# Gated GQA decode step with a gMLP branch: the last head's V load is merged, wo is cut into four loads, and dummy matmuls move

## Chip, cores and metric

One core of a Trainium2 chip runs the whole kernel. The metric is the device time of one execution in microseconds (us); the time of a kernel is the median of several runs.

## The reference, cut to what matters

One token `x` (1 x 1024) goes through two branches that a scalar gate mixes.

```python
def _A_ref(x, k_cache, v_cache, wq, wo):          # 32 query heads, 4 KV heads, 65536 keys, 128 per head
    q = (x @ wq).reshape(B, Sq, Hq, Dh).transpose(0, 2, 1, 3)
    k = jnp.repeat(k_cache, rep, axis=1)           # rep = 8
    v = jnp.repeat(v_cache, rep, axis=1)
    scores = jnp.einsum('bhqd,bhkd->bhqk', q, k) * Dh ** (-0.5)
    p = _softmax(scores, axis=-1)
    o = jnp.einsum('bhqk,bhkd->bhqd', p, v)
    return o.transpose(0, 2, 1, 3).reshape(B, Sq, Hq * Dh) @ wo
...
g = _sigmoid((x * gate_w).sum(-1, keepdims=True))
a = _A_ref(x, A_k_cache, A_v_cache, A_wq, A_wo)
b = _B_ref(x, B_w_in, B_w_sp, B_b_sp, B_w_out)     # a small gMLP block on the same token
return g * a + (1 - g) * b
```

All inputs are bfloat16. The K and V caches are 64 MB each; `wq` and `wo` are 8 MB each, `w_in` 7 MB and `w_out` 3.5 MB. There is one token, so every byte of them is read once and used little.

## The kernel before

**The buffer.** Everything large is loaded by SP's queue (`load`, L177 to L187, issue on L184) into one SBUF buffer `kv` of five slots of 4 MB. A slot holds one tile of a cache: 128 partitions times 128 keys times 128 values. A load names its slot by `at`, which may be a fraction. A load waits until the instructions that used the slot before are done. SP issues in program order, so the order of the loads is written out by hand.

**K tiles** (`k_tile`, L407 on). Each KV head has four K tiles. VectorE (DVE) transposes a tile in place in four parts (L412), TensorE (PE) multiplies it with the query weights `wt` (L419, 32 matmuls of 512 columns), ScalarE (ACT) copies the scores to SBUF (L428). `stats` (L431 on) takes the maximum, the exponentials and their sums and transposes the probabilities into `pt` (L454).

**V tiles** (`v_tile`, L457 on). A V tile needs nothing of DVE: 32 matmuls of 512 columns (L464) with 64 columns of `pt` as weights add to the PSUM tile `o_ps`. After a head's four V tiles `head_out` (L472 on) masks and sums `o_ps` on DVE (L474, L478), adds up over partitions by small matmuls (L482, L484), divides by the softmax sums, multiplies by the gate and writes the head's part of `oa` (L487 to L496).

**The order.** For heads 1 to 3, pairs of K tiles of one head alternate with pairs of V tiles of the head before (L529 to L548). The last head's V tiles come at the end (L549 to L551): tiles 0 and 1 in one load into slots 2 and 3, tile 2 alone into slot 1, tile 3 alone into slot 0. Slots 0 and 1 held V tiles 2 and 3 of the head before.

**The end.** `project` (L511 on) multiplies rows of `wo` with `oa` into `out_ps`: four matmuls of 256 columns (L514) for each of 32 rows, each with a weight load of its own. `wo` comes in as many loads as `WO_SPLIT` has entries, from slot 3 on; so the first, of 24 rows, waits until V tile 1 of the last head has been used. The other loads lie in the upper half of slot 4. Then ACT copies `out_ps` (L566), and two queues write it out (L569).

**Dummy matmuls.** `keep_busy(n)` (L499 to L506) issues `n` matmuls of 512 columns with one weight load (L503) on data that lies in SBUF; their result is never read. Before, there are 6 ahead of the last `head_out`, 16 behind it, and `WO_BUSY[n]` of them behind the `project` of a piece of `n` rows of `wo`.

**Order on each engine.** At the end of the program every instruction is tied to the one before it on its engine (L572 to L579), so each engine runs exactly in the order in which the code is written.

Of the kernel before, what the change touches and what calls it, by code (L numbers as in the profile page):

```python
# [21 lines left out]
CC = CT // VC  # L22
ZN = 448
HN = 512
WO_SPLIT = (24, 4, 2, 1, 1)
WO_BUSY = {24: 0, 4: 2, 2: 1, 1: 0}


@with_exitstack
def kernel(  # L30
# [18 lines left out]
    _, G, S, DH = A_k_cache.shape  # L49
# [15 lines left out]
    assert S % (P * CT) == 0 and F == 2 * NB * ZN and ZN == B * FC and HD == NHB * NB * HN  # L65
    assert NHB * NB == 2 * G and CC * B == 2 * HN and sum(WO_SPLIT) == OC

# [12 lines left out]
    def same_weights(ins):  # L80
        held.add(ins.ins.name)
# [95 lines left out]
    def load(src, shape, at):  # L177
        n = 1
        for s in shape:
            n *= s  # L180
        v = kv[:, int(at * CT * P):int(at * CT * P) + n]
        if len(shape) == 2:
            v = v.rearrange("p (a b) -> p a b", b=shape[1])
        ins = nc.sync.dma_start(out=v, in_=src)  # L184
        if not first_load:
            first_load.append(ins.ins.name)
        return v  # L187

    def load_kv(src, g, j, at, n=1):
        h, i = divmod(j, 2)  # L190
        rows = src[0, g, 2 * h * CT * P:2 * (h + 1) * CT * P, :].rearrange(
            "(p c) d -> p (c d)", c=2 * CT)
        v = load(rows[:, i * CT * DH:(i + n) * CT * DH], (n * CT * DH,), at)
        return [v[:, i * CT * DH:(i + 1) * CT * DH] for i in range(n)]
# [166 lines left out]
    for k in range(NHB):  # L361
# [3 lines left out]
                                                                   j=B, e=2),  # L365
# [91 lines left out]
    def v_tile(g, j, vt):  # L457
        if j == 0:
            o_ps[g] = pso.tile([P, 2, VC * DH], FP32, name="o_ps")
        vx = vt.rearrange("p (v c d) -> p c v d", v=VC, d=DH)  # L460
        for u in range(CC // 2):
            hs = slice(u % 2 * P // 2, (u % 2 + 1) * P // 2)
            for e in range(2):
                ins = nc.tensor.matmul(  # L464
                    o_ps[g][hs, e, :],
                    lhsT=ptt[g, j][:, 2 * u:2 * u + 2, :].rearrange("p c x -> p (c x)"),
                    rhs=vx[:, 2 * u + e], start=(j == 0 and u < 2),
                    stop=(j == NT - 1 and u >= CC // 2 - 2), skip_group_check=True)
                if e > 0:
                    same_weights(ins)  # L470

    def head_out(g):  # L472
        gs = slice(g * B, (g + 1) * B)
        nc.vector.tensor_tensor(  # L474
            out=om8, in0=o_ps[g][:].rearrange("p e (v d) -> p (e v) d", d=DH),
            in1=own_8[:].unsqueeze(2).to_broadcast([P, 2 * VC, DH]), op=ALU.mult)
        o_sb = wk.tile([P, DH], FP32, name="o_sb")
        nc.vector.tensor_reduce(out=o_sb[:], in_=om8.rearrange("p x d -> p d x"), axis=AX.X,  # L478
                                op=ALU.add)
        om_ps = psm.tile([P, DH + NT], FP32, name="om_ps", tag="m")  # L480
        hs = hsel[:].rearrange("p h q -> p (h q)")
        nc.tensor.matmul(om_ps[gs, DH:], lhsT=hs, rhs=lss[g][:], start=True, stop=True,  # L482
                         skip_group_check=True)
        nc.tensor.matmul(om_ps[gs, :DH], lhsT=hs, rhs=o_sb[:], start=True, stop=True,  # L484
                         skip_group_check=True)
        rl = wk.tile([P, 2], FP32, name="rl")
        nc.vector.reduce_sum(out=rl[gs, 0:1], in_=om_ps[gs, DH:], axis=AX.X)  # L487
        nc.vector.reciprocal(out=rl[gs, 1:2], in_=rl[gs, 0:1])
        om = wk.tile([P, QD, OC], FP32, name="om")
        nc.vector.tensor_tensor(  # L490
            out=om[gs], in0=om_ps[gs, :DH].rearrange("p (q c) -> p q c", c=OC),
            in1=own_q[gs, :].unsqueeze(2).to_broadcast([B, QD, OC]), op=ALU.mult)
        osum = wk.tile([P, OC], FP32, name="osum")
        nc.vector.tensor_reduce(out=osum[gs, :], in_=om[gs].rearrange("p q c -> p c q"),
                                axis=AX.X, op=ALU.add)
        nc.vector.tensor_scalar(out=oa[gs, :], in0=osum[gs, :], scalar1=rl[gs, 1:2],  # L496
                                scalar2=gate[gs, :], op0=ALU.mult, op1=ALU.mult)

    def keep_busy(n):  # L499
        ps = pss.tile([P, 2 * HN], FP32, name="busy_ps", tag="s")  # L500
        w = wt[G % 2][:].rearrange("p v b t u h -> p (v b t u h)")
        for i in range(n):
            ins = nc.tensor.matmul(ps[:, :HN], lhsT=w[:, :P], rhs=w[:, :HN], start=True,  # L503
                                   stop=True, skip_group_check=True)
            if i > 0:
                same_weights(ins)  # L506
# [4 lines left out]
    def project(w, n, vec, c0, first=False, last=False):  # L511
        for c in range(n):
            for t in range(NB):
                nc.tensor.matmul(  # L514
                    out_ps[t * B:(t + 1) * B, :],
                    lhsT=vec[:, c0 + c:c0 + c + 1].to_broadcast([P, B]),
                    rhs=w[:, c, t * NO:(t + 1) * NO],
                    start=(first and c == 0), stop=(last and c == n - 1),
                    skip_group_check=True)
# [9 lines left out]
    for g in range(1, G):  # L529
# [16 lines left out]
            if h == 0 and g + 1 < G:  # L546
                build_w(g + 1)
        head_out(g - 1)  # L548
    for j, n, at in ((0, 2, 2), (2, 1, 1), (3, 1, 0)):  # L549
        for i, vt in enumerate(load_kv(A_v_cache, G - 1, j, at, n)):  # L550
            v_tile(G - 1, j + i, vt)  # L551
    keep_busy(6)
    head_out(G - 1)
    keep_busy(16)

# [2 lines left out]
    c0 = 0  # L558
    for n in WO_SPLIT:
        t = load(wo_view[:, c0:c0 + n, :], (n, D), 3 + c0 * D / (CT * P))  # L560
        project(t, n, oa, c0, last=(c0 + n == OC))
        keep_busy(WO_BUSY[n])
        c0 += n
# [46 lines left out]
```

## Time and profile before

| what | value |
|---|---|
| median of 6 runs | 381.89 us (381.71 to 382.03) |
| the profiled execution: its own time | 381.77 us |
| its span in the trace | 380.2 us |
| moved over the span | 162.17 MB, 426 GB/s |
| SP's queue, share of 16 DMA engines' span | 98.8% |
| PE busy / DVE busy / ACT busy | 225.9 / 211.2 / 39.6 us |
| mean granted PE clock | 0.834 |

The span runs from the first to the last instruction of the profiled execution; 1.57 us of its time lie outside it. Times in the views below count from the span's start. "Idle before" or a bracket with an arrow names what ended an engine's wait. The granted clock is 1.00 for PE at full speed and 0.50 for half. Matmuls are pipelined, so their mean duration (411 ns for L464) is longer than the distance from one to the next.

The last landings as the trace tells them by what waited for them: V tiles 0 and 1 at 339.22, tile 2 by 348.93, tile 3 at 358.64, the 24 rows of `wo` at 373.16, the last row at 378.14. The V loads were issued at 312.07 (tiles 0 and 1) and from 330.81 on (tiles 2 and 3), the five `wo` loads from 348.71 to 350.94.

### The profile page before, as it was taken

Reading aid. Unit: us, or ns where it says so; the run is one execution under the profiler, and the core shown is the slowest. Engines: PE = TensorE matmul, PEld = TensorE weight load, DVE = VectorE, ACT = ScalarE, POOL = GpSimd, SP = SyncE. Lnnn points to the kernel's source line nnn. Section 1 sums busy time; section 2 is a strip of 40 time slices with the busy share of each in tenths; the row PEclk is TensorE's granted clock in tenths of the full one; section 3 lists DMA queues with packets and bytes.
Section 4 is the critical chain, followed back from the end, with each engine's and each line's share of the span. In section 5 each row is a group of like instructions: output and inputs, shape, how many; then the busy total and the mean of one; then the engine's idle time right before and its main releaser. Section 6 shows DMA issues by size and latency. Waiting matters only on the chain.

```text
span 380.2 us, 2602 instructions
## 1 busy us (share of the span) xinstructions
PE 225.9 (59%) x1397; PEld 55.4 (15%) x800; DVE 211.2 (56%) x207; ACT 39.6 (10%) x55; POOL 4.4 (1%) x10
## 2 busy tenths in 40 slices
PE   0050604967746794794499229762993197739386
PEld 0010100211201210121022001110220011202113
DVE  4152217989474946867893058679940397650040
ACT  1001000111103300114011001140110010500000
POOL 4000000000000000000000000000000000000000
PEclk9995655999958796999599758996899589959889
DMA  9998999999999999999999999999999999999995
GB/s 386 483 434 379 415 442 441 434 480 437 400 408 434 441 436 441 427 441 441 434 436 441 441 434 434 393 429 442 427 441 429 421 441 442 436 403 438 424 439 229
DMA packets 3655, 162.17 MB, mean 426 GB/s; under 512 B 440, under 2 KB 444, under 8 KB 828
## 3 DMA queue, kind: packets, MB, share of 16 engines
q1 hardware_dynamic: 3604, 162.01, 98.8%
q8 instruction: 8, 0.13, 0.1%
q14 instruction: 3, 0.02, 0.0%
q10 hardware_dynamic: 40, 0.01, 0.0%
HBM read 162.01 MB, written 0.00 MB: 426 GB/s over the span
## 4 chain that ended last, share of the span: by engine, by line
DMA 64%; PE 19%; DVE 12%; issue 3%; ACT 1%; SPq 0%; ACTq 0%; DVEq 0%
DMA kv<-in_A_k_cache_dram 45%; PE s_ps L419 14%; DVE kv L412 10%; DMA kv<-in_A_wo_dram 7%; DMA kv<-in_A_v_cache_dram 7%; DMA wb<-in_B_b_sp_dram 5%; PE o_ps L464 3%; DVE pt L454 1%; PE z_ps L296 1%; DVE o_sb L478 0%; SPq L184 0%; DVE mx L402 0%; ACT sc L451 0%; DVE rowt L474 0%; ACT sc L428 0%
## 5 line engine op out<-in xcount | busy, mean ns | idle before, releaser
L419 PE MATMUL s_ps<-kv,wt 128*128 128x512 bf16 x512 | 133.1, 415 | 80.7 <-DVE kv L412 80.6
L412 DVE STREAM_TRANSPOSE kv<-kv 128x2048 int32<-128x2048 int32 x64 | 142.4, 2280 | 69.3 <-DMA kv<-in_A_k_cache_dram 69.3
L464 PE MATMUL o_ps<-kv,pt 128*64 128x512 bf16 x512 | 64.1, 411 | 14.2 <-DMA kv<-in_A_v_cache_dram 14.2
L419 PEld LDWEIGHTS <-wt 128*128 128x128 bf16 x256 | 26.4, 103 | 188.8 <-issue 117.3
L428 ACT CAST sc<-s_ps 128x1024 bf16<-128x1024 f32 x16 | 16.2, 1012 | 252.4 <-PE s_ps L419 252.4
L464 PEld LDWEIGHTS <-pt 128*64 128x64 bf16 x256 | 17.0, 118 | 58.0 <-issue 48.7
L454 DVE STREAM_TRANSPOSE pt<-sc 128x1024 bf16<-128x1024 bf16 x16 | 18.6, 1217 | 6.8 <-ACT sc L451 6.8
L474 DVE TENSOR_TENSOR rowt<-o_ps,own 128x1024 f32<-128x1024 f32 x4 | 4.8, 1195 | 26.8 <-PE o_ps L464 26.8
L451 ACT ACTIVATE sc<-sc,nb 128x1024 bf16<-128x1024 bf16 x16 | 18.2, 1138 | 12.2 <-DVE nb L447 12.2
L484 PE MATMUL om_ps<-o_sb,hsel 128*32 128x128 f32 x8 | 2.3, 386 | 18.3 <-DVE o_sb L478 18.3
L402 DVE TENSOR_TENSOR mx<-mx,sc 128x1024 bf16<-128x1024 bf16 x8 | 5.5, 687 | 13.7 <-ACT sc L428 13.7
L296 PE MATMUL q_ps<-kv,xT 128*32 128x512 bf16 x64 | 6.0, 555 | 8.9 <-DMA kv<-in_A_wq_dram 8.9
L363 DVE TENSOR_TENSOR rowt<-q_ps,own_b 128x512 f32<-128x512 f32 x2 | 1.3, 687 | 12.7 <-PE q_ps L296 12.7
L252 PE MATMUL xb_ps<-xg,spread 8*128 8x256 bf16 x1 | 0.4, 368 | 13.3 <-DMA xg<-in_gate_w_dram 13.3
L478 DVE TENSOR_REDUCE o_sb<-rowt 128x128 f32<-128x1024 f32 x4 | 7.5, 1871 | 0.1
L503 PE MATMUL busy_ps<-wt 128*128 128x512 bf16 x25 | 6.1, 381 | 0.0
L566 ACT CAST out_sb<-out_ps 128x256 bf16<-128x256 f32 x1 | 0.4, 372 | 46.4 <-PE out_ps L514 46.4
L256 DVE TENSOR_TENSOR xm<-xb_ps,sel_i 128x128 f32<-128x128 f32 x2 | 0.5, 286 | 8.1 <-PE xb_ps L252 8.1
L435 DVE TENSOR_REDUCE m<-mx 128x1 f32<-128x1024 bf16 x4 | 4.8, 1210 | 0.1
L514 PE MATMUL out_ps<-kv,oa 128*32 128x256 bf16 x128 | 4.2, 273 | 1.1 <-DMA kv<-in_A_wo_dram 1.1
L296 PEld LDWEIGHTS <-xT 128*32 128x32 bf16 x64 | 2.5, 130 | 15.7 <-issue 15.7
L296 PE MATMUL z_ps<-kv,xT 128*32 128x448 bf16 x64 | 4.7, 464 | 0.0
(90 smaller groups left out, 60.9 us busy)
## 6 DMA issues: line engine op xcount, KB each, us to landing
kv<-in_A_v_cache_dram SPq DMA_DIRECT2D x2, 4096.0 KB, 22.7
kv<-in_B_w_in_dram SPq DMA_DIRECT2D x1, 7168.0 KB, 19.5
kv<-in_A_wo_dram SPq DMA_DIRECT2D x1, 6144.0 KB
kv<-in_B_w_out_dram SPq DMA_DIRECT2D x1, 3584.0 KB
kv<-in_A_wo_dram SPq DMA_DIRECT2D x1, 1024.0 KB, 26.6
kv<-in_A_wo_dram SPq DMA_DIRECT2D x1, 512.0 KB
kv<-in_A_wo_dram SPq DMA_DIRECT2D x2, 256.0 KB
kv<-in_A_k_cache_dram SPq DMA_DIRECT2D x8, 27.5
```

The lines of the kernel that those rows point to most:

```text
L296: ins = nc.tensor.matmul(ps[t * B:(t + 1) * B, k * HN:k * HN + n], lhsT=xT[:, i * KH + c:i * KH + c + 1].to_broadcast([P, B]), rhs=w[:, c, ...
L402: nc.vector.tensor_tensor(out=mx[:], in0=mxs[g][:], in1=sc[:], op=ALU.max)
L412: nc.vector.transpose(out=kb[:, v * n:(v + 1) * n], in_=kb[:, v * n:(v + 1) * n])
L419: ins = nc.tensor.matmul(s_ps[:, k * HN:(k + 1) * HN], lhsT=wt[g % 2][:, v, b].rearrange("p a v h -> p (a v h)"), rhs=kx[:, b // 2, b % 2, ...
L428: nc.scalar.copy(out=sct[g, j][:], in_=s_ps[:])
L435: nc.vector.reduce_max(out=m1[:], in_=mxs[g][:], axis=AX.X)
L451: nc.scalar.activation(out=sct[g, j][:], in_=sct[g, j][:], func=ACT.Exp, scale=SCALE, bias=nb[:, 0:1], accum_out=lss[g][:, j:j + 1])
L454: nc.vector.transpose(out=ptt[g, j][:].rearrange("p c x -> p (c x)"), in_=sct[g, j][:])
L464: ins = nc.tensor.matmul(o_ps[g][hs, e, :], lhsT=ptt[g, j][:, 2 * u:2 * u + 2, :].rearrange("p c x -> p (c x)"), rhs=vx[:, 2 * u + e], sta ...
L474: nc.vector.tensor_tensor(out=om8, in0=o_ps[g][:].rearrange("p e (v d) -> p (e v) d", d=DH), in1=own_8[:].unsqueeze(2).to_broadcast([P, 2 ...
L478: nc.vector.tensor_reduce(out=o_sb[:], in_=om8.rearrange("p x d -> p d x"), axis=AX.X, op=ALU.add)
L503: ins = nc.tensor.matmul(ps[:, :HN], lhsT=w[:, :P], rhs=w[:, :HN], start=True, stop=True, skip_group_check=True)
```

## The change

The last head's V tiles 2 and 3 come in one load of 8 MB, into slots 0 and 1. `wo` comes in 24, 6, 1 and 1 rows, no longer in 24, 4, 2, 1 and 1. Twenty-four dummy matmuls are issued behind V tile 1. The 6 ahead of the last `head_out` and the 16 behind it stay. Behind the 24 rows of `wo` come 2 dummies where there were none, and behind the later pieces none where there were 2 and 1. DVE, ACT and POOL run the same instructions in the same order; PE runs as many `project` matmuls as before.

```diff
@@ -22,8 +22,8 @@
-WO_SPLIT = (24, 4, 2, 1, 1)
-WO_BUSY = {24: 0, 4: 2, 2: 1, 1: 0}
+WO_SPLIT = (24, 6, 1, 1)
+WO_BUSY = {24: 2, 6: 0, 1: 0}
@@ -546,10 +546,10 @@
         head_out(g - 1)
-    for j, n, at in ((0, 2, 2), (2, 1, 1), (3, 1, 0)):
-        for i, vt in enumerate(load_kv(A_v_cache, G - 1, j, at, n)):
+    for j, at in ((0, 2), (2, 0)):
+        for i, vt in enumerate(load_kv(A_v_cache, G - 1, j, at, 2)):
             v_tile(G - 1, j + i, vt)
-    keep_busy(6)
+        keep_busy((24, 6)[j // 2])
     head_out(G - 1)
     keep_busy(16)
```

## The prediction

> **What bounds the kernel now.** I read first the table of queues and the chain of waits in order of time, to learn whether transfers or engines set the end; then the timeline of the last 45 us; then PE's clock, window by window. The chain's last entries:
>
> ```profile
> 312.07 27.11 DMA kv<-in_A_v_cache_dram
> 339.22 9.48 PE o_ps L464 x64
> 348.71 0.33 SPq L184
> ...
> 350.51 27.63 DMA kv<-in_A_wo_dram
> 378.18 0.32 PE out_ps L514 x4
> 378.52 0.37 ACT out_sb L566
> ```
>
> SP's transfers fill 98.8% of 16 DMA engines' span, and the end is the landing of the last wo row (378.14), four matmuls and the output. PE and DVE cost nothing so long as they are ready when wo lands. How nearly they are late is read in the timeline:
>
> ```profile
> 339.22 9.45 PE L464 MATMUL o_ps<-kv,pt 128*64 128x512 bf16 x64 [2.11 <-DMA kv<-in_A_v_cache_dram]
> ...
> 348.93 3.65 PE L464 MATMUL o_ps<-kv,pt 128*64 128x512 bf16 x32 [0.26 <-DMA kv<-in_A_v_cache_dram]
> ...
> 358.64 6.52 PE L464 MATMUL o_ps<-kv,pt 128*64 128x512 bf16 x32 [6.07 <-DMA kv<-in_A_v_cache_dram]
> ...
> 368.73 3.63 PE L503 MATMUL busy_ps<-wt 128*128 128x512 bf16 x16
> ...
> 373.16 3.24 PE L514 MATMUL out_ps<-kv,oa 128*32 128x256 bf16 x112 [0.81 <-DMA kv<-in_A_wo_dram]
> ```
>
> The rows are V tiles 0 and 1, tile 2, tile 3, the 16 dummies, and the first project. Tile 2 takes 3.65 us and tile 3, the same 32 matmuls, 6.52. From the end of tile 3 (365.16) the path is head_out on DVE and PE to 368.73, then the dummies to 372.36: 7.20 us. PE then waits 0.8 us for wo's 24 rows. That 0.8 us is all the slack there is. The clock explains the two durations (columns: window; its length; busy time of PE, PEld, DVE, ACT, POOL with counts; granted clock; DMA share; GB/s):
>
> ```profile
> 118.74:122.15 3.41, 1.15 (x7) 0.37 (x3) 0.65 (x3) 2.28 (x2) 0.00 (x0) 1.00 1.29 557
> 122.15:125.56 3.41, 0.00 (x0) 0.13 (x1) 2.11 (x2) 3.40 (x7) 0.00 (x0) 0.50 0.80 346
> 159.70:163.11 3.41, 1.54 (x8) 0.31 (x4) 3.41 (x2) 0.00 (x0) 0.00 (x0) 1.00 1.25 538
> 163.11:166.52 3.41, 2.81 (x13) 0.55 (x6) 2.79 (x2) 0.00 (x0) 0.00 (x0) 1.00 0.80 346
> 350.84:354.25 3.41, 1.73 (x17) 0.54 (x7) 0.00 (x0) 0.00 (x0) 0.00 (x0) 1.00 1.00 432
> 354.25:357.67 3.42, 0.00 (x0) 0.00 (x0) 0.00 (x0) 0.00 (x0) 0.00 (x0) 1.00 0.99 426
> 357.67:361.08 3.41, 2.44 (x12) 0.81 (x7) 0.00 (x0) 0.00 (x0) 0.00 (x0) 0.50 0.97 418
> 361.08:364.49 3.41, 3.41 (x18) 0.91 (x8) 0.00 (x0) 0.00 (x0) 0.00 (x0) 0.50 1.07 461
> 364.49:367.91 3.42, 2.23 (x14) 0.23 (x3) 2.67 (x2) 0.00 (x0) 0.00 (x0) 1.00 1.06 460
> ```
>
> All 22 changes of the granted clock in this span lie on one grid of 3.413 us, so I cut windows on it. Each change follows the window just ended: full clock was kept after windows with PE busy 45% or more (159.70) and lost after 34% (118.74) or less; half clock was kept up to 72% (357.67) and left from 77% on. Tile 3 is slow because PE stood idle 6.07 us before it.
>
> **The change, part by part.** *Loads.* V tiles 2 and 3 become one 8 MB load into slots 0 and 1. Both loads before were issued together at 330.81, released by the same PE step, so the start doesn't move. 8 MB took 19.42 us as two loads (339.22 to 358.64), and 19.36 each as the two single loads before them (300.50 to 339.22): a gain of 0.06. But tile 2's first matmul, ready at 348.93 before, now waits until 358.6; behind it on PE stand all 64 matmuls, the dummies and head_out, and DVE's L474 waits for them. SP issues four wo loads for five (about 0.43 us each, over 27 us ahead of the last landing: hidden); the first still waits for tile 1's last matmul, which stands ahead of the new dummies, so wo goes out at 348.7 as before. wo's landings stay: the 24 rows at 373.16, the last at about 378.1.
>
> *Dummies after tile 1.* From the rows of 16 (3.63) and 6 (1.47), one more costs 0.216 us and a train 0.39 - 0.216 on top: 24 take 5.35 us. From 348.61 they end at 353.96. PE is idle then, so by themselves they cost nothing. But the wait ends at 358.64: 4.68 us stay unfilled, more than a whole window of 3.41.
>
> *Tiles 2 and 3 together.* Four matmuls take 0.853 us at half clock (weight loads at 340.50 and 341.36) and 0.433 at full (345.27, 345.70): 0.213 and 0.108 each. So 64 take 64 x 0.108 + 0.19 = 7.11 us at full clock, and each us spent at half clock adds 0.49. Test on tiles 0 and 1: 4.81 us of half clock (339.22 to 344.03) give 9.48, measured 9.45. With c the time at half clock, the tiles end at 358.64 + 7.11 + 0.49c = 365.75 + 0.49c, and PE is free for project 7.20 later, at 372.95 + 0.49c.
>
> *How long the clock is low.* A gap of 4.68 us lying as evenly as it can over two windows leaves each 31% busy, under the 34% that lost the clock; so I take it as lost wherever the grid lies. That 34% window held some very small matmuls, hence a rival below. Where the grid lies against the kernel this one trace can't tell, so I let it lie anywhere. With x from 353.96 to the next grid point, the loss after a window over 2.05 us idle (between 34 and 45% busy) and the recovery after one under 0.85 idle (between 72 and 77%): x under 0.42 (12%) gives c = 5.6 to 6.0; to 1.27 (25%) 2.6 to 3.4; to 2.05 (23%) 3.4; the rest (40%) 4.2 to 5.6. Mean 4.2. This profile's own grid (x = 0.29) would give 5.85.
>
> [...]
>
> *Project.* 24 rows are 96 matmuls at 0.0283 (112 took 3.17 until the next train); two dummies 0.61 (376.33 to 376.94); the last 8 rows, landed by then, 32 x 0.0283 = 0.91; the last matmul's tail 0.17. Together 4.41. Before, dummies 2 + 1 cost 0.93, hidden by the wait for the last row; now the 0.61 is on the path. End of the last matmul: 372.95 + 0.49c + 4.41 = 377.36 + 0.49c, against 378.47 before: 0.49c - 1.11. With c of 2.6 to 6.0 that is +0.2 to +1.8, at the mean +0.95; tiles 0 and 1's own c of 4.81 gives +1.26. What follows the last matmul is the same. The profiled execution took 381.77 (span 380.2), 0.12 under the median, so 381.89 + 0.95 = 382.8.
>
> **Rivals.** *The clock holds* (the other side: not slower). If a window has to be nearly empty before the clock falls, part of the grid positions keep it. It decides at about 31% of a window: if that keeps the clock, c is 0 for some positions. PE is then free at 372.95, ahead of the landing at 373.16, the 24 rows and two dummies end at 376.5, the last row lands at 378.1, and the time is 381.7 to 381.9. For: the 34% window counts about 0.6 us of tiny matmuls, so full-size work of 34% was never seen to lose the clock. Against: 27% (101.67), 17% (330.36) and 4% all lost it, which leaves few positions.
>
> *The loads gain* (faster). From 375.5 on the rate falls to 340, 225, 205, 123 and 8 GB/s in half-us slices: against 433, 632 KB are missing, 1.46 us. If larger pieces (6 rows for 4 and 2) cured all of it, and the clock held, PE would bound at 377.36: -1.1 us, 380.8. Against: 8 MB of wo took 358.64 to 378.14 = 19.50 us, against 19.36 for 8 MB of V, so small pieces cost at most 0.14; the ragged end looks like engines that finish apart, which the change leaves alone.
>
> *The clock stays low through both tiles.* 64 x 0.213 + 0.19 = 13.8 us, the tiles end at 372.5, the 22 dummies stay half as fast, and it is +6 or more. Against: no dense stretch in this trace stayed low for over 5.9 us (109.47 to 115.33, 358.64 to 364.51).
>
> **How the numbers follow.** About 0.2%, 0.76 us, can be told from no change. The clock lost: 0.85. Half of its positions lie above +0.76 and half below, with most of the weight of the upper half well above; a median of several executions stays nearer +0.95 than the ends, so 0.59 slower and 0.26 within. The clock holds: 0.10, within. The loads gain: 0.04. Low throughout: 0.01, slower. Sum: slower 0.60, same 0.36, faster 0.04. The range takes in c from 2.6 to 6.0 and the upper end of "the clock holds": 381.9 to 383.7.
>
> **What would show it.** Right: wo's 24 rows land at about 373.2 and PE starts project later than that with no DMA wait before L514, at 374 to 376; the 64 matmuls of tiles 2 and 3 take 8.4 to 10 us with granted clock 0.50 for part of it; an idle 4.7 us after the 24 dummies; the last matmuls wait for nothing; single times of the changed kernel scatter more than the 0.32 us of before. Wrong: clock 1.00 all the way from 344 to the end and an L514 wait for the last row; or wo landing at another time than now; or a gap after the dummies much shorter than 4.7.

## The result, and the profile after

| | median | lowest to highest | runs |
|---|---|---|---|
| before | 381.90 us | 381.71 to 382.23 | 42 |
| changed | 382.85 us | 381.84 to 383.93 | 21 |

The ratio is 1.0023, with a 95% interval of 1.0017 to 1.0029. The medians lie 0.95 us apart, as forecast (382.8), and the spread grew from 0.5 us to 2.1: the middle half of the changed kernel's runs lies between 382.27 and 383.20. In the three longest of the changed runs (383.68 to 383.93) 2.1 to 2.4 us lie outside the span, in the other 18 1.4 to 1.6; what that means stands under "What stays open".

The profiled execution took 381.65 us (span 380.2), 1.2 us under the median of its kernel and less than the fastest of the 21. It must be read as that. The end of its chain:

```profile
330.87 27.71 DMA kv<-in_A_v_cache_dram
358.62 8.40 PE o_ps L464 x64
367.04 1.24 DVE rowt L474
368.30 1.88 DVE o_sb L478
...
370.23 0.41 PE om_ps L484 x2
370.63 3.56 PE busy_ps L503 x16
374.19 2.73 PE out_ps L514 x96
376.93 0.54 PE busy_ps L503 x2
377.46 1.01 PE out_ps L514 x32
378.50 0.37 ACT out_sb L566
```

Before, this chain ended in a transfer of wo and four matmuls. Now no transfer follows the V landing at 358.62: the merged tiles, head_out, the 16 dummies, the whole project and the 2 dummies in it follow each other on PE and DVE, and wo waits for them. Even in this fast execution PE sets the end. The rows of PE in the timeline (the bracket is the idle time before and what ended it):

```profile
348.71 5.35 PE L503 MATMUL busy_ps<-wt 128*128 128x512 bf16 x24
...
358.62 8.38 PE L464 MATMUL o_ps<-kv,pt 128*64 128x512 bf16 x64 [4.55 <-DMA kv<-in_A_v_cache_dram]
...
374.12 2.80 PE L514 MATMUL out_ps<-kv,oa 128*32 128x256 bf16 x96
```

The 24 dummies last 5.35 us and leave 4.55 us idle. The first project starts at 374.12 with no wait for wo; before it started at 373.16 after a wait. The clock, in windows on the grid of 3.413 us (columns as in the prediction):

```profile
351.02:354.43 3.41, 3.05 (x15) 0.11 (x1) 0.00 (x0) 0.00 (x0) 0.00 (x0) 1.00 1.02 442
354.43:357.85 3.42, 0.00 (x0) 0.00 (x0) 0.00 (x0) 0.00 (x0) 0.00 (x0) 1.00 0.83 359
357.85:361.26 3.41, 2.64 (x14) 0.82 (x7) 0.00 (x0) 0.00 (x0) 0.00 (x0) 0.50 0.93 404
361.26:364.67 3.41, 3.41 (x35) 1.12 (x16) 0.00 (x0) 0.00 (x0) 0.00 (x0) 1.00 1.03 447
```

The dummies kept the clock to 357.85; the unfilled rest lost it up to 361.26. The merged tiles start at 358.62, so they have 2.64 us of half clock (c), the lower end of what was forecast.

### The profile page after: what moved, and what is told of

It is laid out like the page before. It is cut to its first block, busy times and chain, and to the rows that moved or that the text cites. A ratio compares the mean times of both kernels' runs of the same rounds, so it can differ in the third digit from the quotient of the medians.

```text
span 380.2 us, 2622 instructions
## 1 busy us (share of the span) xinstructions
PE 229.7 (60%) x1420; PEld 55.1 (14%) x800; DVE 211.2 (56%) x207; ACT 39.6 (10%) x55; POOL 4.4 (1%) x10
## 4 chain that ended last, share of the span: by engine, by line
DMA 57%; PE 23%; DVE 15%; issue 3%; ACT 1%; ACTq 0%; DVEq 0%
DMA kv<-in_A_k_cache_dram 45%; PE s_ps L419 14%; DVE kv L412 11%; DMA kv<-in_A_v_cache_dram 7%; PE o_ps L464 5%; DMA wb<-in_B_b_sp_dram 5%; DVE pt L454 1%; PE busy_ps L503 1%; DVE o_sb L478 1%; PE out_ps L514 1%; PE z_ps L296 1%; DVE rowt L474 1%; ACT sc L428 1%; DVE mx L402 1%; ACT sc L451 0%
## 5 line engine op out<-in xcount | busy, mean ns | idle before, releaser
L464 PE MATMUL o_ps<-kv,pt 128*64 128x512 bf16 x512 | 62.5, 404 | 13.2 <-DMA kv<-in_A_v_cache_dram 13.2
L464 PEld LDWEIGHTS <-pt 128*64 128x64 bf16 x256 | 16.7, 117 | 60.5 <-issue 51.3
L503 PE MATMUL busy_ps<-wt 128*128 128x512 bf16 x48 | 11.1, 380 | 0.0
L514 PEld LDWEIGHTS <-oa 128*32 128x32 bf16 x128 | 3.3, 96 | 4.0 <-issue 3.9
```

The costliest lines, as they stand in the source:

```text
L464: ins = nc.tensor.matmul(o_ps[g][hs, e, :], lhsT=ptt[g, j][:, 2 * u:2 * u + 2, :].rearrange("p c x -> p (c x)"), rhs=vx[:, 2 * u + e], sta ...
L514: nc.tensor.matmul(out_ps[t * B:(t + 1) * B, :], lhsT=vec[:, c0 + c:c0 + c + 1].to_broadcast([P, B]), rhs=w[:, c, t * NO:(t + 1) * NO], st ...
```

## The experiments

Every kernel below was compared with the kernel before on the same chip; its median there was 381.76 us for the first eight and 381.83 for the last two. The theory is that of the prediction. The rivals: the dummies cost by themselves (A), they hold the clock in part of the runs (B), the merged load costs whatever the clock (C), the wo pieces carry the cost (D), a window has to be idle as a whole before the clock falls (E), the clock falls already near 45% busy or above (F).

### Without the 24 dummies

```diff
-        keep_busy((24, 6)[j // 2])
+        keep_busy((0, 6)[j // 2])
```

> The changed kernel without the 24 dummies behind V tile 1: PE stands idle for about 9.9 us before the merged tiles, not 4.6. Theory (the clock is lost in any gap whose idleness exceeds about 2.05 us in one 3.413 us window, and 4.6 us is already too long): the clock is lost as before, half clock c of 2.6 to 6.0 us by where the grid lies, mean 4.3; the time is that of the changed kernel, 382.8 (381.9 to 383.7 for the median), single runs from 381.9 to 383.7. Rival A (the 24 dummies themselves cost, by delaying PE or the transfers): 381.9, and little scatter. Rival B (the 24 dummies do hold the clock in part of the runs): clearly slower than the changed kernel, by 0.3 us or more.

Measured: 383.02 us (382.06 to 383.53, 11 runs), ratio 1.0024 (1.0015 to 1.0033). That is the changed kernel's ratio: the 24 dummies neither cost nor help by an amount that the ratios show, so A falls as the cause of the added time. B asked for 0.3 us or more; the medians stand 1.26 us above before here and 0.95 in the changed kernel, and with intervals of 0.2 to 0.3 us to either side that much can't be told apart. The profiled execution was the longest of the 11, 383.53 us, and shows the other end of c:

```profile
347.68:351.09 3.41, 1.29 (x12) 0.34 (x5) 0.00 (x0) 0.00 (x0) 0.00 (x0) 1.00 0.98 423
351.09:354.51 3.42, 0.00 (x0) 0.00 (x0) 0.00 (x0) 0.00 (x0) 0.00 (x0) 0.50 1.11 479
...
357.92:361.33 3.41, 2.40 (x12) 0.82 (x7) 0.00 (x0) 0.00 (x0) 0.00 (x0) 0.50 1.03 447
361.33:364.75 3.42, 3.42 (x18) 0.93 (x8) 0.00 (x0) 0.00 (x0) 0.00 (x0) 0.50 1.06 460
364.75:368.16 3.41, 3.41 (x34) 1.08 (x16) 0.00 (x0) 0.00 (x0) 0.00 (x0) 1.00 1.00 432
```

Its first window lost the clock at 38% busy, with L464 matmuls and nothing else in it: the next one is at 0.50. The window from 357.92, 2.40 us or 70% busy, did not bring it back, where 2.64 us did in the changed kernel: 0.24 us more of work saved that execution a window of 3.4 us. The chain puts the difference where the prediction's sum has it:

```profile
358.93 9.96 PE o_ps L464 x64
...
376.07 2.73 PE out_ps L514 x96
```

### 42 dummies: the gap is filled

```diff
-        keep_busy((24, 6)[j // 2])
+        keep_busy((42, 6)[j // 2])
```

> The changed kernel with 42 dummies behind V tile 1 in place of 24: they take 9.2 us and end at about 357.9, which leaves PE idle for only 0.7 us. Theory (the added time is half clock alone): clock 1.00 from 344 to the end, tiles 2 and 3 in 7.1 us, PE ahead of wo's 24 rows by a hair, 381.8 to 382.0, and the scatter of single runs falls from 2 us to about 0.4. Rival C (the merged load costs by itself, since 64 matmuls and not 32 follow the last V landing): 0.5 us or more above the kernel before, whatever the clock. Rival A (dummies cost): slower than the changed kernel.

Measured: 381.67 us (381.49 to 382.90), ratio 1.0001 (0.9993 to 1.0010). The added time is gone with the load still merged, so rivals A and C fall as its cause. In the timeline of this execution the gap is 0.36 us, the 64 matmuls run at full clock, and wo is waited for again:

```profile
358.61 7.10 PE L464 MATMUL o_ps<-kv,pt 128*64 128x512 bf16 x64 [0.36 <-DMA kv<-in_A_v_cache_dram]
...
373.14 2.80 PE L514 MATMUL out_ps<-kv,oa 128*32 128x256 bf16 x96 [0.25 <-DMA kv<-in_A_wo_dram]
```

The expected scatter of 0.4 us was not met: nine runs lie between 381.49 and 381.86, the other two at 382.47 and 382.90. These two have spans of 380.1 and 380.3 us, as the nine have; their excess lies outside the span.

### The wo pieces and their dummies alone

```diff
-WO_SPLIT = (24, 4, 2, 1, 1)
-WO_BUSY = {24: 0, 4: 2, 2: 1, 1: 0}
+WO_SPLIT = (24, 6, 1, 1)
+WO_BUSY = {24: 2, 6: 0, 1: 0}
```

This is an edit of the kernel before; all other kernels here are edits of the changed one.

> The kernel before with the change's wo pieces (24, 6, 1, 1 rows) and its 2 dummies behind the 24 rows; the V loads and the 6 and 16 dummies stay as before. Theory: PE is ahead of wo, the 2 dummies are hidden by the wait for the 6 rows, the last landing stays: 381.8 to 382.0. Rival D (the wo pieces carry the cost): 382.4 or more. If larger pieces shorten the ragged end of the transfers: below 381.7.

Measured: 381.73 us (381.56 to 381.84), ratio 0.9998 (0.9990 to 1.0007). Rival D falls, and so does the hope of a shorter ragged end: the last four matmuls start at 378.06, against 378.18 before.

### 6 dummies, not 16, between head_out and project

```diff
-    keep_busy(16)
+    keep_busy(6)
```

> The changed kernel with 6 dummies behind the last head_out in place of 16. The clock is lost as in the changed kernel, but head_out to project takes 5.0 us in place of 7.2. Theory (half clock costs only what the path behind it has no slack for, and the 16 dummies are on that path): PE is free for project at 370.8 + 0.49c, at c of 6.0 at 373.7, so the last wo row sets the end again: 381.8 to 382.0, with the L464 row of 64 still 8.4 to 10 us. Rival C (the merged tiles cost by themselves, behind wo): 382.4 or more.

Measured: 381.68 us (381.57 to 381.94), ratio 0.9998 (0.9989 to 1.0007). Here the clock is lost and nothing is added:

```profile
358.62 9.44 PE L464 MATMUL o_ps<-kv,pt 128*64 128x512 bf16 x64 [5.18 <-DMA kv<-in_A_v_cache_dram]
...
371.62 1.47 PE L503 MATMUL busy_ps<-wt 128*128 128x512 bf16 x6
373.16 2.80 PE L514 MATMUL out_ps<-kv,oa 128*32 128x256 bf16 x96
...
378.12 0.29 PE L514 MATMUL out_ps<-kv,oa 128*32 128x256 bf16 x4 [0.31 <-DMA kv<-in_A_wo_dram]
```

The tiles took 9.44 us, over a us more than in the profile of the changed kernel, and still the last wo row sets the end. So the 4.78 us of half clock in the tiles cost nothing here: with 6 dummies before wo (1.47 us) in place of 16 (3.63) the path had the slack for them. In the changed kernel the dummies that were to keep the clock had eaten it.

### 32 and 37 dummies: how long a gap loses the clock

```diff
-        keep_busy((24, 6)[j // 2])
+        keep_busy((32, 6)[j // 2])
```

and the same with 37.

> The changed kernel with 32 dummies behind V tile 1: they take 7.1 us and leave PE idle for about 2.9 us, less than one window of 3.413 us. Theory (a window loses the clock when it is idle for more than about 2.05 us): some grid positions put over 2.05 of the 2.9 us into one window and lose it, others split the gap and hold it; the time lies between the kernel before and the changed one, 382.0 to 382.5, with single runs from 381.7 to 383.5. Rival E (a window has to be idle as a whole): the clock is never lost, 381.6 to 381.9 with a scatter under 0.5 us.

> The changed kernel with 37 dummies behind V tile 1: they take 8.2 us and leave PE idle for about 1.8 us. Theory: no grid position puts over 2.05 us of idleness into one window, the clock holds always, 381.6 to 381.9, and tiles 2 and 3 take 7.1 us. Rival F (the clock falls at less idleness than that, near 45% busy or above): part of the runs at 382.0 and more, as some of the run with 42 were.

Measured: with 32, 381.79 us (381.37 to 382.68), ratio 1.0000 (0.9991 to 1.0008); with 37, 381.92 us (381.45 to 382.30), ratio 1.0004 (0.9995 to 1.0013). The median with 32 missed its expected 382.0 to 382.5: the clock is lost less often, or for less long, than I had put it. The times can't tell which: the profiled execution ran 2.62 us of the tiles at half clock and still took 381.68. Rival E fails all the same, by the profile of the kernel with 32, where a gap of 2.83 us lost the clock:

```profile
354.45:357.86 3.41, 1.36 (x7) 0.11 (x1) 0.00 (x0) 0.00 (x0) 0.00 (x0) 1.00 0.92 399
357.86:361.27 3.41, 2.62 (x14) 0.81 (x7) 0.00 (x0) 0.00 (x0) 0.00 (x0) 0.50 0.87 375
```

The first window holds 1.36 us of dummies, 40% busy, and the next one runs at half clock. With 37, a gap of 1.42 us kept it (window 354.97 to 358.38, 62% busy). The median with 37 lies a hair above the expected 381.9; within the interval it is no change. Three of its runs lie at 382.27 to 382.30, where rival F expected some. Two of them have spans of 380.1 and 380.2 us, so no clock made them long; one has 380.9. That one is no sign for F either: PE is free for the dummies up to 1.3 us earlier in other traces (see "The grid's place"), and by an estimate from that the gap left by 37 dummies reaches 2.7 us, near the 2.83 that lost the clock with 32.

### The merged load alone

```diff
-WO_SPLIT = (24, 6, 1, 1)
-WO_BUSY = {24: 2, 6: 0, 1: 0}
+WO_SPLIT = (24, 4, 2, 1, 1)
+WO_BUSY = {24: 0, 4: 2, 2: 1, 1: 0}
...
-        keep_busy((24, 6)[j // 2])
+        keep_busy((0, 6)[j // 2])
```

> The merged V load alone: wo in 24, 4, 2, 1 and 1 rows with 2 and 1 dummies behind the 4 and the 2 as before, no dummies behind V tile 1, 6 and 16 around the last head_out. Theory: the whole added time comes from here; as in the run without the 24 dummies, and the small pieces' 3 dummies (0.93 us, now on the path) add 0.3 to it against the 2 of the changed kernel (0.61): 1.0 + 0.3 above the kernel before, 382.9 to 383.4. Rival D (the wo pieces carry a part): no more than 382.5.

Measured: 383.04 us (382.11 to 383.63), ratio 1.0027 (1.0017 to 1.0036). With the wo part at nothing, the merge carries the whole. The extra 0.3 us of its third dummy can't be told in the times (383.04 against 383.02 without the 24 dummies), but the trace has 0.43: from the first project to the end of the last matmul 4.76 us (374.13 to 378.89) against 4.33 (374.12 to 378.45).

### 42 and 6: a miss, and the other use of the dummies

```diff
-        keep_busy((24, 6)[j // 2])
+        keep_busy((42, 6)[j // 2])
...
-    keep_busy(16)
+    keep_busy(6)
```

> The changed kernel with 42 dummies behind V tile 1 and 6 in place of 16 behind the last head_out: the clock holds and the path has 2.2 us of slack. Theory: the transfers alone set the end, 381.6 to 381.8, and the few single runs of 382.5 and 382.9 that the run with 42 showed are gone, since they were PE being late by a hair with no slack. If those came from something else than PE's lateness, they stay.

Measured: 382.21 us (381.51 to 383.23), ratio 1.0010 (1.0001 to 1.0018). I expected the best of all, and the median is above that of either edit alone. The profile, of an execution of 382.21 us, shows one reason:

```profile
369.45:372.87 3.42, 1.31 (x6) 0.09 (x1) 1.15 (x5) 0.00 (x0) 0.00 (x0) 1.00 0.78 327
372.87:376.28 3.41, 3.11 (x60) 2.71 (x63) 0.00 (x0) 0.00 (x0) 0.00 (x0) 0.50 0.89 363
```

```profile
373.17 4.30 PE L514 MATMUL out_ps<-kv,oa 128*32 128x256 bf16 x96 [2.41 <-DMA kv<-in_A_wo_dram]
```

PE is early now, stands idle for 2.41 us before wo, and loses the clock there (38% busy). Project takes 4.30 us in place of 2.80, and the last matmul ends at 379.0. In the profile with 6 dummies and the clock lost earlier, PE came late and had no such gap.

This is half of the miss. The profiled execution has a span of 380.8 us, and four of the 11 runs have one of 380.6 to 380.9; the other seven have 380.1 or 380.2, no more than before. Eight runs took over 382 us: three are long inside the span, four outside it (2.0 to 2.3 us there, against 1.4 to 1.6 in the others), and one, of 383.23 us, both. So the long single runs stayed, as expected if PE's lateness was not behind them.

### 42 and 13 dummies, with 16 and with 12

```diff
-        keep_busy((24, 6)[j // 2])
+        keep_busy((42, 13)[j // 2])
```

and, in the second kernel, also

```diff
-    keep_busy(16)
+    keep_busy(12)
```

> The changed kernel with 42 dummies behind V tile 1, and 13 in place of 6 behind tile 3: the 13 take 3.0 us and end just before DVE's sum that head_out's matmuls wait for, so that no gap of PE over 0.5 us is left between 348.6 and wo. Theory (the few slow single runs with 42 and 37 dummies are half clock too, lost in a window that takes in the 1.7 us gap in head_out): 381.5 to 381.8 and no run above 382.1. If they come from elsewhere: again one run in five above 382.2.

> As the run with 42, 13 and 16 dummies, but 12 in place of 16 behind the last head_out: PE is free for project at about 372.0, 1.1 us ahead of wo's 24 rows, and idle for no more than that. Theory: the transfers alone set the end, 381.5 to 381.8, with the smallest scatter of all variants of the changed kernel, and not more than 0.3 us faster than the kernel before, since the last landing is not moved. If a slack of 0.25 us was what let the slow single runs through, they are gone here and not in the run with 16.

Measured: 381.74 us (381.57 to 382.59), ratio 0.9999 (0.9990 to 1.0008), and 381.65 us (381.51 to 382.44), ratio 0.9999 (0.9990 to 1.0008). In both profiles the merged tiles take 7.10 us and the last matmuls wait for wo. So neither is faster than before: with no delay by PE the transfers set the end where they did (378.08 and 378.10). The guess on the long single runs failed twice: two of 11 still lie above 382.2 in each, with the gap in head_out filled (0.18 us left) and with 1.1 us of slack. All four have spans of 380.1 to 380.5 us, which says that half clock is not what makes them long. With 12, gaps are left: 1.71 us before the merged tiles and 1.10 before wo, and the clock held in both.

## Why the prediction was right

**The bound and the transfers.** Right. V landed at 358.62 (forecast 358.6), the first wo load left behind tile 1 as before, and where PE was early wo's 24 rows landed at 373.14 and the last row at 378.1. The wo split by itself is worth nothing that can be measured.

**The gap.** Right. 24 dummies took 5.35 us as worked out, and 4.55 us stayed open (forecast 4.68).

**Half clock in the merged tiles.** Right, and the best tested term: 7.11 + 0.49c, with c read from the granted clock.

| kernel | c, us | 7.11 + 0.49c | measured |
|---|---|---|---|
| 42 dummies | 0 | 7.11 | 7.10 |
| changed | 2.64 | 8.40 | 8.38 |
| merged load alone | 2.90 | 8.53 | 8.51 |
| 6 before wo | 4.78 | 9.45 | 9.44 |
| no dummies | 5.82 | 9.96 | 9.95 |

All five values lie in the forecast's cases (none, or 2.6 to 6.0).

**The rival "the clock holds".** It rested on one doubt, the tiny matmuls in the 34% window. Windows of full-size work settled it: 38% (no dummies, and again 42 and 6) and 40% (32 dummies) lost the clock. The even split at 31% is well below these.

**The grid's place.** The prediction let it lie anywhere, for want of a second trace. PE has the same work in all of these kernels up to 347 us, and still the grid point near 357 lay at 357.67 (before), 357.85 (changed), 357.92 (no dummies) and 356.57 (6 before wo). So it lay differently in each of these executions. Rival E, a whole idle window, fails on the changed kernel too: a gap of 4.55 us, as in its profile, would hold a whole window of 3.413 us in a third of the grid's positions (an estimate from these two numbers), so the 24 dummies would have left most runs at the time of before, and 3 of 21 were within 0.1 us of it; and gaps of 2.41 us (42 and 6) and 2.83 us (32 dummies) lost the clock.

One step here was simpler than the traces are. The prediction moved the grid and kept the end of tiles 0 and 1 at 348.61. But the grid also sets the half clock of those tiles: over the twelve traces they spent 2.80 to 5.60 us in it and took 8.46 to 9.85 us, so PE was free for the dummies anywhere from 347.64 to 349.01. The same 24 dummies left 4.55 us in one trace and 5.18 in another, 42 dummies left 0.36 or 1.71. The cases of the prediction are thus not as likely as it put them. Moving both together gives by an estimate from these rows a mean c of 4.3, against its 4.2; that the mean hardly moves is luck.

**Sizes that were off.** Two terms were a little long: from the end of the tiles to project 7.12, not 7.20, and project to the end 4.33, not 4.41, together 0.16 us; with them mended the mean is +0.79, so a median of just +0.95 is partly luck. The single runs spread from -0.1 to +2.0 us around the median of before, where c alone gives +0.2 to +1.8, or +0.0 to +1.7 with those two terms mended. Without the three runs that are long outside the span they spread from -0.1 to +1.4.

**The chances.** "Slower" was put at 0.60 because the mean of +0.95 us stands close to the bound of 0.76. The median came out at +0.95, above it; the ratio's interval reaches down to 1.0017, below it.

**What stays open.** The kernels with 42, 37, and 42 with 13 dummies have the median of before, but two or three of their 11 runs each at 382.2 to 382.9 (of 129 runs of before three were above 382.2, the highest 382.49). I took them for half clock in some other place. The spans on record speak against that: eight of these nine runs have a span of 380.1 to 380.5 us, as the others have, and 2.0 to 2.6 us of time outside it. So neither a wait nor a slower clock between the first and the last instruction made them long. Such a time outside goes with the dummies behind V tile 1: it is there in 17 of 98 runs of the kernels that have 24 to 42 of them (three of 21 of the changed kernel, none of 11 with 6 before wo), and in none of 120 runs without them (87 of the kernel before; 33 with the wo pieces alone, the merged load alone or no dummies there), where at most 1.57 us lie outside. So dummies do seem to cost something in some runs, and in this form rival A was not ruled out. What happens in that time, and whether the dummies cause it, no trace here shows.

## What to carry to other kernels

A load split in two isn't only a matter of transfer size: the first half let work start early here (tile 2 at 348.93 us, merged at 358.62), and the split kept 32 matmuls off the path behind the last landing, which the transfers' own time (0.06 us) could not show. Dummy matmuls had to fill most of the gap here: 24 of them, which left 4.55 us and more idle, gave nothing measurable, while 32, which left 2.83 in the profile, brought the median back to that of before. On the path behind a late step dummies were a delay themselves (3.56 us of the chain for 16 of them), so weigh them against the slack at that place. Where, as here, the clock changes on a grid that lies differently in each execution (the point near 357 from 356.57 to 357.92), give times as a spread and take many runs: one profile shows one case, here the fastest of all. And set each run's time beside its span: a run that is long outside the span can't be explained by anything in a trace.

## What the runs showed of the hardware

In these traces the granted clock went with the busy share of the window just ended, and the edge was narrow. The figures here are those of before and of the changed kernel from 23 us on, where its record begins, and those of the other ten where slices of 0.25 us cover them. All changes of the clock there lie on a grid of 3.413 us, each trace with its own, which makes 589 windows. Every window at full clock with PE busy 39% or less lost it and every one from 46% on kept it; between 40 and 45% both happened (1.46 us of 3.41 kept it in the trace with 42 dummies, from 314.10; 1.53 lost it in that with 6 before wo, from 117.64), so the busy share as the trace counts it doesn't tell these apart. At half clock every window of 78% and more brought full clock back and none up to 75% did; at 77% both happened (2.62 us brought it back with 32 dummies, from 357.86, and did not without the 24 dummies, from 60.95). In the merged tiles 2.40 us of work left the next 3.4 us at half clock (no dummies) and 2.64 us did not (changed), a difference of 0.24 us.

A wait of 2.41 us just before the 96 matmuls on wo's first piece (42 and 6) went with 1.5 us more in them (4.30 us in place of 2.80, the granted clock at 0.50 up to 376.28), and in that execution the last matmul ended at 379.0, where with 42 and 16 dummies it ended at 378.4: this gap, slack by the forecast, cost more than the ten dummies that it replaced.

The time of a run and the span of its instructions are not the same thing. Over the 218 runs for which the record has both, 1.37 to 1.76 us lie outside the span in 201 and 2.03 to 2.63 in 17, all 17 with 24 or more dummies behind V tile 1.
